# The last expert's first tile of rows, weighed and scattered in two halves of its columns

## The chip, the cores and the metric

The kernel runs on one core of a Trainium2 chip. The metric is the device time of one execution in microseconds. All arithmetic on the main path is in float32.

## What is computed

An attention block without a softmax is followed by a mixture of experts that leaves some rows alone. Cut to what matters here:

```python
kv  = einsum('bhsd,bhse->bhde', k, v)
o   = einsum('bhsd,bhde->bhse', q, kv)
x   = o / sqrt(mean(o*o, -1) + 1e-6) * g_norm     # rows: 4608 x 512
out = x.copy()
for the rows with x @ w_skip > 0:
    e      = argmax(x @ w_gate)                   # one of 8 experts
    gate_w = softmax(x @ w_gate)[e]
    h      = relu(x @ w1[e])                      # 512 -> 1024
    out[row] = x + gate_w * (h @ w2[e])           # 1024 -> 512
```

## The kernel before

The first part of the program computes x, writes it to the output in DRAM, and gives every chosen row a slot at its expert. The second part goes through the experts one after the other, those with most rows first (`experts`, L1428). For each expert, GpSimd gathers the rows from DRAM into a tile `xg` (128 partitions; a chunk `c` of 512 columns holds one row on each partition), TensorE turns them, multiplies by w1 (layer 1), and multiplies the hidden values by w2 (layer 2). What comes out of layer 2 for a tile of 128 rows stands in one PSUM bank of 128 x 512 values. VectorE weighs it: a `scalar_tensor_tensor` computes `x = gate * bank + x` in `xg` (in `result`, L1381). GpSimd then scatters the rows to their places in DRAM with an indirect DMA (L1384), which takes the row numbers from a table.

Layer 2 for the first 256 rows of an expert is `fast_2` (L1326). It uses a scheme of Winograd's kind: the 256 rows, the hidden values and the columns are halved, and seven products of half size take the place of eight, with some sums on VectorE in between. `X` is the bank of the first tile of rows and `Y` that of the second; `lo` and `hi` are the two halves of a bank's columns, 256 each. A product (`product`, L1251) is four matmuls over the hidden values, which the trace shows as eight records each of matmul and of weight load. The order in which the source issues the work is the order on every engine (the schedule is written out by hand), so TensorE does these products one after the other as they stand in `fast_2`: X lo, Y lo, X hi, Y lo again, X lo again (L1361), X hi again (L1363), and Y lo a last time (L1368). X hi gets an `add` (L1364) before it is final. `held` copies half a bank to SBUF on ScalarE.

`put` calls `result` for a whole tile. `part` is a second way out of a bank, used in the last expert alone (r = E - 1, L1488): it calls `half_result` (L1400), which weighs one half of the columns (L1404) and scatters it as half rows of 256 values (L1407). Its row numbers, twice the row number plus the half, come from the table `two`, built by `half_rows` (L1391) in the second expert's turn for both tiles and both halves. Before the change, only Y goes out this way: its `hi` half right after its add (L1359) and its `lo` half after the very last product (L1370). X goes out whole through `put` (L1365). The last expert has exactly 256 rows of room, so `rest` (L1366) is empty for it, and it has no sums of a next expert to do (`do(work, ...)` finds an empty list).

All scatters of one pass stand in a group within which the program declares no order between them (L1388, L1411), since each row has one slot. GpSimd issues them in the order of the source.

Of the kernel before, what the change touches and what calls it, by code (L numbers as in the profile page):

```python
# [17 lines left out]
def kernel(  # L18
# [47 lines left out]
    P = 128  # L66
# [940 lines left out]
    for n in range(NU + 2):  # L1007
# [31 lines left out]
        for pace, stream in streams:  # L1039
            for job in itertools.islice(stream, pace):  # L1040
                if job:
                    part, job = job if isinstance(job, tuple) else ("pe", job)
# [9 lines left out]
    with tc.tile_pool(name="wpool_b", bufs=1, reuse_waits="tile") as wpool_b, \  # L1052
# [6 lines left out]
        def bank():  # L1059
            return ps_b.tile([P, 512], FP32, tag="bank", name="bank")  # L1060
# [116 lines left out]
        def layer_2(r, ht, piece, yps=None, fs=range(FC)):  # L1177

            off, m = piece[0:2]
            n = DM * m // P  # L1180
            ht = ht if callable(ht) else (lambda f, all=ht: all[:, f, :])
            yps = yps or bank()
            for f in fs:
                for q in range(P // m):
                    nc.tensor.matmul(out=yps[q * m:(q + 1) * m, 0:n], lhsT=ht(f)[:, off:off + m],  # L1185
                                     rhs=w_sb[r][1][:, f, q * n:(q + 1) * n],
                                     start=(f == 0), stop=(f == FC - 1), skip_group_check=True)
            return yps
# [56 lines left out]
        def do(work, n=None):  # L1245
            n = len(work) if n is None else min(n, len(work))
            for job in work[:n]:
                job()
            del work[:n]

        def product(out, k, lhsT, rhs, start):  # L1251
            for i in range(k):
                nc.tensor.matmul(out=out, lhsT=lhsT(i), rhs=rhs(i), start=start and i == 0,  # L1253
                                 stop=i == k - 1, skip_group_check=True)

        def add(to, x, y):
            nc.vector.tensor_tensor(out=to, in0=x, in1=y, op=ALU.add)  # L1257

        def held(x, tag):

            n = x.shape[-1]
            t = ffn.tile([P, 256], FP32, tag=tag, name=tag)[:, 0:n]
            nc.scalar.copy(out=t, in_=x)  # L1263
            return t
# [61 lines left out]
        def fast_2(r, ht, rest, work, put, part=None):  # L1326

            w2, s, t = w_sb[r][1], sums.pop((r, "h")), sums.pop((r, "w2"))
            lo, hi = slice(0, HM), slice(HM, DM)

            def h(j, m):
                return lambda f: ht[:, j * HF + f, m * P:(m + 1) * P]

            def hs(i):
                return lambda f: s[:, i, f, :]

            def w(j, ds):
                return lambda f: w2[:, j * HF + f, ds]

            def ws(i):  # L1340
                return lambda f: t[:, i, f, :]

            X, Y = bank(), bank()
            product(X[:, lo], HF, h(0, 0), w(0, lo), True)
            p1 = held(X[:, lo], "p1")
            do(work, 3)
            product(Y[:, lo], HF, hs(1), ws(1), True)
            add(Y[:, lo], Y[:, lo], p1)  # L1350
            u = held(Y[:, lo], "u")
            do(work, 3)
            product(X[:, hi], HF, hs(0), ws(0), False)
            p5 = held(X[:, hi], "p5")
            do(work, 2)
            product(Y[:, lo], HF, h(0, 1), ws(2), False)
            add(Y[:, hi], Y[:, lo], p5)
            if part:
                part(1, 1, Y)  # L1359
            do(work, 2)  # L1360
            product(X[:, lo], HF, h(1, 0), w(1, lo), False)  # L1361
            do(work, 2)
            product(X[:, hi], HF, hs(2), w(1, hi), False)  # L1363
            add(X[:, hi], X[:, hi], u)  # L1364
            put((0, P), X)  # L1365
            for piece in rest:  # L1366
                put(piece[0:2], layer_2(r, ht, piece))
            product(Y[:, lo], HF, h(1, 1), ws(3), False)  # L1368
            if part:
                part(1, 0, Y)  # L1370
            else:
                put((P, P), Y)
            do(work)
# [54 lines left out]
        def experts(pieces, widths, srcs, xt, ht, yps0, tables, group):  # L1428

            for r in range(E):  # L1430
# [36 lines left out]
                if r == 0:  # L1467
                    if yps0 is None:
                        gather_all(2, pieces, *srcs)
                    ys = [bank() for _ in todo]  # L1470
                    for fs in (range(HF), range(HF, FC)):
                        for piece, y in zip(todo, ys):
                            layer_2(r, ht, piece, y, fs)
                    do(beside, 4)
                    for piece, y in zip(todo, ys):
                        result(piece, y, xgs[r], tables, group)
                    do(beside)
                else:
                    if yps0 is not None and r == 1:
                        rnd_i = rounds()  # L1480
                    if yps0 is not None and r == E - 1:
                        n_rounds.append(nc.values_load(rnd_i[0:1, 0:1], min_val=1,
                                                       max_val=ROUNDS + 1))
                    of = {piece[0:2]: piece for piece in todo}
                    part = None
                    if yps0 is not None and r == 1:
                        two = half_rows(tables[0][0])
                    if yps0 is not None and r == E - 1:  # L1488
                        part = lambda c, half, y: half_result(c, half, y, xgs[r], two,
                                                              tables[0][1], group)  # L1490
                    fast_2(r, ht, todo[2:], beside,
                           lambda key, y: result(of[key], y, xgs[r], tables, group), part)
# [136 lines left out]
```

## Time and profile before

| | us |
|---|---|
| time, median of 3 runs | 376.25 (375.22 to 376.61) |
| the profiled execution's own time | 376.26 |
| its span, first to last instruction | 374.40 |
| TensorE busy in matmuls | 363.2 |
| VectorE busy | 244.3 |
| ScalarE busy | 146.0 |
| GpSimd busy | 123.1 |

The span is shorter than the time, since the time takes in what lies before the first and after the last instruction. In the profile, PE is TensorE's matmuls and PEld its weight loads, which overlap them; DVE is VectorE, ACT is ScalarE, POOL is GpSimd. A row names the line, the engine, the operation, the tiles written and read by the program's names (all PSUM tiles of the second part are called `bank`), and in square brackets how long the engine had been idle and whose work ended that. The ends of matmuls are modelled. The granted clock of TensorE was 0.996 of full speed over the span.

The rows that matter for the change are those of the last 12 us. Layer 2 of the last expert begins on TensorE at 356.6 us. The last scatter of the program starts at 370.05 us and takes GpSimd 0.98 us; the rest of the span, to 374.40, is the landing of its bytes and the end of the program.

### The profile page before, as it was taken

To read this page: it belongs to the slowest core of one execution; us is meant where nothing else is said; L and a number is where in the kernel's file an instruction comes from. 1 tells how busy PE (TensorE), PEld (TensorE's weight loads), DVE (VectorE), ACT (ScalarE), POOL (GpSimd) and SP (SyncE) were. 2 spreads that over 40 slices of the span, in tenths; PEclk is the share of its full clock that TensorE was granted. 3 is DMA by queue.
4 is the path that set the end of the run, shared out by engine and by line. 5 is a ranking of instruction groups with operands and counts; after the bars stand their busy time and mean duration, and the time that the engine had idled before them with its cause. 6 is when DMAs were issued, how large, how long until landed. Compare 5 with 4: busy or idle time off the path is not lost.

```text
span 374.4 us, 9661 instructions
## 1 busy us (share of the span) xinstructions
PE 363.2 (97%) x3859; PEld 315.2 (84%) x3859; DVE 244.3 (65%) x627; ACT 146.0 (39%) x398; POOL 123.1 (33%) x191
## 2 busy tenths in 40 slices
PE   8999999999999999999999999999999999999994
PEld 4687797898979679779879987988998998998983
DVE  2354458667878845676766675876876876878831
ACT  2366676676776222214403421430440440441420
POOL 7035457655768555223012303203202302102003
PEclk9999999999999999999999999999999999999998
DMA  7999999996499449966518263672762761700001
GB/s 290 393 391 391 401 403 394 404 384 201 130 330 311 111 109 325 395 204 226 203 53 268 69 226 103 225 254 54 259 228 47 273 230 61 269 3 32 26 1 53
DMA packets 32039, 81.70 MB, mean 218 GB/s; under 512 B 2474, under 2 KB 2482, under 8 KB 31988
## 3 DMA queue, kind: packets, MB, share of 16 engines
q1 hardware_dynamic: 28176, 69.47, 52.3%
q0 software_dynamic: 3792, 11.53, 9.2%
q8 instruction: 32, 0.52, 0.6%
q14 instruction: 19, 0.16, 0.1%
q10 hardware_dynamic: 20, 0.02, 0.0%
HBM read 66.80 MB, written 14.48 MB: 217 GB/s over the span
## 4 chain that ended last, share of the span: by engine, by line
PE 83%; issue 6%; POOL 4%; DVE 3%; ACT 3%; POOLq 0%; DVEq 0%; ACTq 0%
PE bank L1253 44%; PE bank L1185 9%; PE o_ps L498 7%; PE sum_ps L379 5%; PE bank L1173 4%; PE q_ps L460 3%; PE g_ps L393 2%; PE q_ps L170 2%; PE bank L1154 2%; POOL xb L615 2%; DVE xl L545 1%; DVE rs L522 1%; PE g_ps L411 1%; ACT qT L463 1%; ACT sq L514 1%
## 5 line engine op out<-in xcount | busy, mean ns | idle before, releaser
L1263 ACT COPY p<-bank 128x128 f32<-128x128 f32 (+6 forms) x70 | 20.8, 297 | 99.5 <-PE bank L1253 88.2
L1253 PE MATMUL bank<-xt,w 128*128 128x128 f32 (+5 forms) x336 | 55.5, 288 | 0.0
L615 POOL TENSOR_TENSOR xb<-xl,g_b 128x512 f32<-128x512 f32 x36 | 43.7, 1216 | 34.3 <-DVE rs L536 30.4
L1384 POOL DMA_INDIRECT out_dram<-xg,rows x14 | 14.0, 999 | 118.6 <-DVE xg L1381 115.4
L1253 PEld LDWEIGHTS bank<-xt,w 128*128 128x128 f32 x336 | 47.0, 190 | 1.9 <-DVE bank L1257 1.4
L1257 DVE TENSOR_TENSOR bank<-bank,p 128x128 f32<-128x128 f32 (+6 forms) x70 | 23.6, 338 | 30.2 <-PE bank L1253 29.0
L498 PE MATMUL o_ps<-kvd,qT 128*128 128x146 f32 x240 | 35.8, 290 | 1.0 <-ACT kvd L415 0.7
L1253 PE MATMUL bank<-xs,s 128*128 128x128 f32 (+5 forms) x224 | 36.7, 289 | 0.0
L522 DVE TENSOR_REDUCE rs<-sq 128x8 f32<-128x512 f32 x36 | 24.6, 682 | 15.6 <-ACT sq L514 15.5
L498 PEld LDWEIGHTS o_ps<-kvd,qT 128*128 128x128 f32 x240 | 31.6, 188 | 2.0 <-ACT kvd L415 1.5
L1253 PEld LDWEIGHTS bank<-xs,s 128*128 128x128 f32 x224 | 31.1, 190 | 1.0 <-ACT p L1263 0.8
L1185 PE MATMUL bank<-w,ht 128*32 128x128 f32 (+2 forms) x424 | 29.9, 313 | 0.0
L545 DVE TENSOR_TENSOR xl<-o_ps,rs 128x584 f32<-128x584 f32 x32 | 24.5, 767 | 4.3 <-DVE rs L536 0.5
L1185 PEld LDWEIGHTS bank<-w,ht 128*32 128x32 f32 (+2 forms) x424 | 18.2, 119 | 10.7 <-issue 7.6
L1253 PE MATMUL bank<-t,ht 128*128 128x256 f32 x112 | 27.0, 384 | 0.0
L1145 POOL DMA_INDIRECT xg<-out_dram,src x14 | 15.6, 1116 | 33.3 <-DMA out_dram<-xg,rows 18.0
L1253 PE MATMUL bank<-w,ht 128*128 128x256 f32 x112 | 26.5, 380 | 0.0
L514 ACT ACTIVATE sq<-o_ps 128x512 f32<-128x512 f32 x34 | 20.3, 597 | 15.0 <-PE o_ps L498 14.4
L379 PE MATMUL sum_ps<-v,k 64*64 64x64 f32 x1152 | 25.3, 227 | 0.4 <-issue 0.4
L1253 PE MATMUL bank<-t,hs 128*128 128x256 f32 x112 | 25.3, 379 | 0.0
L379 PEld LDWEIGHTS sum_ps<-v,k 64*64 64x64 f32 x1152 | 21.4, 138 | 4.5 <-issue 2.2
L1253 PEld LDWEIGHTS bank<-t,ht 128*128 128x128 f32 x112 | 20.8, 190 | 3.9 <-issue 1.2
(223 smaller groups left out, 679.2 us busy)
## 6 DMA issues: line engine op xcount, KB each, us to landing
w<-in_moe_w_dram SPq DMA_DIRECT2D x16, 2048.0 KB, 8.9
k<-in_k_dram SPq DMA_DIRECT2D x16, 576.0 KB, 9.9
v<-in_v_dram SPq DMA_DIRECT2D x16, 576.0 KB, 10.7
q<-in_q_dram SPq DMA_DIRECT2D x16, 576.0 KB, 10.2
out_dram<-xb SPq DMA_DIRECT2D x29, 256.0 KB, 9.8
out_dram<-xb POOLq DMA_DIRECT2D x7, 256.0 KB, 6.6
xg<-out_dram,src POOLq DMA_INDIRECT x16, 3.6
out_dram<-xg,rows POOLq DMA_INDIRECT x16, 6.2
```

Of the source, the lines that this page charges most:

```text
L379: nc.tensor.matmul(out=sum_ps[w * 64:(w + 1) * 64, a, u, :], lhsT=kt[r, 2 * u + w, c, :], rhs=vt[r, 2 * u + w, c, :], start=(c == 0), stop ...
L498: mm = nc.tensor.matmul(out=ps[:, w, 0:2 * PK].rearrange("p (r k) -> p r k", r=2)[:, :, cols], lhsT=qT[:, w, a, :], rhs=kvds[b % KVD][:, u ...
L514: nc.scalar.activation(out=sq[:, :, :, :], in_=heads(ps, G, G + 2 * D), func=ACT.Square)
L522: nc.vector.tensor_reduce(out=rs[:, :, :], in_=sq[:, :, :, :].rearrange("p x y (a d) -> p x (y a) d", a=2), axis=AX.X, op=ALU.add)
L545: nc.vector.tensor_tensor(out=xl[:, :, :, :].rearrange("p x y (a k) -> p x (y a) k", a=2), in0=ps[:, :, 0:2 * PK].rearrange("p x (h k) -> ...
L615: late.append((lambda: nc.gpsimd.tensor_tensor(out=xb[:, :, 4 * u * D:(4 * u + 4) * D].rearrange("p r (w x) -> p r w x", w=2), in0=xl[:, : ...
L1145: nc.gpsimd.indirect_dma_start(out=x_of(xg, off, m), out_offset=None, in_=cut_rows(m)[:, :], in_offset=bass.IndirectOffsetOnAxis(ap=idx[:, ...
L1173: nc.tensor.matmul(out=hps[:, cols], lhsT=w_sb[r][0][:, dc, f * P:(f + 1) * P], rhs=xt[:, dc, cols], start=(dc == 0), stop=(dc == DC - 1))
L1185: nc.tensor.matmul(out=yps[q * m:(q + 1) * m, 0:n], lhsT=ht(f)[:, off:off + m], rhs=w_sb[r][1][:, f, q * n:(q + 1) * n], start=(f == 0), s ...
L1253: nc.tensor.matmul(out=out, lhsT=lhsT(i), rhs=rhs(i), start=start and i == 0, stop=i == k - 1, skip_group_check=True)
L1257: nc.vector.tensor_tensor(out=to, in0=x, in1=y, op=ALU.add)
L1263: nc.scalar.copy(out=t, in_=x)
```

## The change

In the last expert, X also goes out in two halves. Its `lo` half is weighed and scattered directly after the second product into X lo, ahead of the product into X hi; its `hi` half is weighed and scattered after the add, where `put` sent out the whole tile. In all other experts `part` is None and nothing differs.

```diff
             do(work, 2)
             product(X[:, lo], HF, h(1, 0), w(1, lo), False)
+            if part:
+                part(0, 0, X)
             do(work, 2)
             product(X[:, hi], HF, hs(2), w(1, hi), False)
             add(X[:, hi], X[:, hi], u)
-            put((0, P), X)
+            if part:
+                part(0, 1, X)
+            else:
+                put((0, P), X)
             for piece in rest:
                 put(piece[0:2], layer_2(r, ht, piece))
             product(Y[:, lo], HF, h(1, 1), ws(3), False)
```

What `part` calls was there before:

```python
        def half_result(c, half, yps, xg, two, gate, group):
            ds = slice(half * HM, (half + 1) * HM)
            col = (E - 1) * CK + c
            nc.vector.scalar_tensor_tensor(
                out=xg[:, c, ds], in0=yps[:, ds], scalar=gate[:, col:col + 1], in1=xg[:, c, ds],
                op0=ALU.mult, op1=ALU.add)
            ins = nc.gpsimd.indirect_dma_start(
                out=cut_rows(P // 2)[:, :],
                out_offset=bass.IndirectOffsetOnAxis(ap=two[:, c, half:half + 1], axis=0),
                in_=xg[:, c, ds], in_offset=None, bounds_check=2 * N - 1, oob_is_err=False)
            tc.declare_no_dep(ins.ins, group=group, reason="each row has one slot")
            tc.add_to_no_dep_group(group, ins.ins)
```

## The prediction

> **What bounds the kernel now.** I read the page's first and fourth part, then the timeline of the last 25 us, since the changed lines run once, in the last expert, then the timelines of two earlier places where TensorE waits for another engine's access to a PSUM bank, and last the windows and landings of the final stores. The page first:
>
> ```profile
> PE 363.2 (97%) x3859; PEld 315.2 (84%) x3859; DVE 244.3 (65%) x627; ACT 146.0 (39%) x398; POOL 123.1 (33%) x191
> ...
> PE 83%; issue 6%; POOL 4%; DVE 3%; ACT 3%; POOLq 0%; DVEq 0%; ACTq 0%
> ```
>
> TensorE is the bound nearly throughout: 97% busy and 83% of the chain that ended last. Any wait added on TensorE ahead of its last matmul moves the end almost one for one, unless something after it has slack. Whether it has, the timeline of the end shows (start us, us, engine, line, operation, names, shapes, count, idle before and who ended it):
>
> ```profile
> 363.61 1.89 PE L1253 MATMUL bank<-w,ht 128*128 128x256 f32 x8
> 363.88 0.43 DVE L1257 TENSOR_TENSOR bank<-bank,p 128x256 f32<-128x256 f32 x1 [3.02 <-PE bank L1253]
> 364.34 0.48 DVE L1404 SCALAR_TENSOR_TENSOR xg<-bank,gate,xg 128x256 f32<-128x256 f32 x1
> 365.10 0.98 POOL L1407 DMA_INDIRECT out_dram<-xg,rows  x1 [19.43 <-DVE xg L1404]
> 365.12 1.70 PEld L1253 LDWEIGHTS bank<-w,hs 128*128 128x128 f32 x8
> 365.33 1.89 PE L1253 MATMUL bank<-w,hs 128*128 128x256 f32 x8
> 366.84 1.70 PEld L1253 LDWEIGHTS bank<-t,ht 128*128 128x128 f32 x8
> 367.06 1.89 PE L1253 MATMUL bank<-t,ht 128*128 128x256 f32 x8
> 367.26 0.43 DVE L1257 TENSOR_TENSOR bank<-bank,u 128x256 f32<-128x256 f32 x1 [2.43 <-PE bank L1253]
> 367.73 0.75 DVE L1381 SCALAR_TENSOR_TENSOR xg<-bank,gate,xg 128x512 f32<-128x512 f32 x1
> 368.76 0.98 POOL L1384 DMA_INDIRECT out_dram<-xg,rows  x1 [2.67 <-DVE xg L1381]
> 368.99 0.48 DVE L1404 SCALAR_TENSOR_TENSOR xg<-bank,gate,xg 128x256 f32<-128x256 f32 x1 [0.51 <-PE bank L1253]
> 370.05 0.98 POOL L1407 DMA_INDIRECT out_dram<-xg,rows  x1 [0.30 <-issue]
> ```
>
> Three products of eight matmul records end it: X lo (363.61 to 365.50), X hi (365.33 to 367.22), Y lo (367.06 to 368.95); each starts 1.73 us after the one before. X is finished by an add (L1257), weighed whole (L1381, 512 columns, 0.75 us) and scattered at 368.76. Y lo is weighed from 368.99 to 369.47. A scatter starts 0.28 us after the weighing it waits for (364.82 to 365.10; 368.48 to 368.76), so Y lo's could start at 369.75. It starts at 370.05, because GpSimd is in X's scatter until 369.74 and the next one follows 0.31 us later. So the end is set by X's chain through GpSimd's queue, with Y lo's own chain 0.30 us behind. After that last scatter ends at 371.03, 3.37 us remain to the span's end at 374.40.
>
> The windows of the end say whether the bytes matter:
>
> ```profile
> 369.70:370.00 0.30, 0.00 (x0) 0.00 (x0) 0.00 (x0) 0.00 (x0) 0.04 (x1) 1.00 0.00 0
> ...
> 370.30:370.60 0.30, 0.00 (x0) 0.00 (x0) 0.00 (x0) 0.00 (x0) 0.30 (x1) 1.00 1.08 369
> 370.60:370.90 0.30, 0.00 (x0) 0.00 (x0) 0.00 (x0) 0.00 (x0) 0.30 (x1) 1.00 0.98 355
> ...
> 371.50:371.80 0.30, 0.00 (x0) 0.00 (x0) 0.00 (x0) 0.00 (x0) 0.00 (x0) 0.50 0.69 256
> ```
>
> The last two columns are DMA share and GB/s. X's 256 KB move at 370.3 to about 371.0, Y lo's 128 KB at about 371.4 to 371.9: the engines are free again before the last scatter's bytes come, so moving X's bytes earlier shortens nothing behind it.
>
> **What the Trainium skill says.** "PSUM — Partial Sum Buffer", section "PSUM bank collisions raise a hardware error": two engines must not access one bank and partition quadrant at the same time, even at disjoint columns, and the guard is to be by bank, not by address. X lo and X hi are two halves of one bank, and the new weighing reads X lo while TensorE's next product writes X hi. The trace of before shows that this kernel is guarded so. At an expert's start, ACT copies X lo, and the product into X hi of the same bank waits for that read:
>
> ```profile
> 232.21 0.27 ACT L1263 COPY p<-bank 128x134 f32<-128x134 f32 x1 [10.79 <-PE bank L1253]
> 232.53 0.53 PEld L1253 LDWEIGHTS bank<-xs,s 128*128 128x128 f32 x4 [0.16 <-ACT p L1263]
> ```
>
> and with VectorE, at the end of layer 1, the product into X lo waits for the add on X hi (355.11 + 0.30 = 355.41; weights at 355.47):
>
> ```profile
> 355.11 0.30 DVE L1257 TENSOR_TENSOR bank<-bank,u 128x128 f32<-128x128 f32 x1
> 355.47 0.52 PEld L1253 LDWEIGHTS bank<-xt,w 128*128 128x128 f32 x4 [0.21 <-DVE bank L1257]
> ```
>
> In both, the weight load begins 0.05 to 0.06 us after the other engine ends; it waits too, so nothing is preloaded. "SBUF — State Buffer", section "Who interferes with whom": a VectorE instruction with one SBUF input does not contend with GpSimd. The trace agrees: L1404 takes 0.48 us alone (364.34) and inside a scatter (368.99). "DMA: Bandwidth & Descriptors", section "Anatomy of one DMA", puts a fixed cost of about 2.0 us on a GpSimd DMA, mostly completion; here issue to landing was 2.9, 3.2 and 2.4 us for the last three scatters, so it stays a constant behind the last one.
>
> **The change part by part.**
>
> Added: one L1404 weighing of X lo straight after its product, and its scatter. VectorE is idle then (364.82 to 367.26), so its own 0.48 us is free there: 365.54 to 366.02, starting 0.04 us after the product's end as at 368.95 to 368.99. Its scatter would be ready at 366.30; GpSimd is in Y hi's until 366.08, plus 0.31 makes 366.39, to 367.37. GpSimd is idle until 368.76 now, so its 0.98 us is hidden.
>
> Added wait: the X hi product is the next thing on TensorE's queue and, by the rule above, stands until 366.02; Y lo stands behind it, and both of their weighings and scatters behind that. Weight load at 366.02 + 0.05 = 366.07; from an idle array the first matmul follows its load by about 0.10 us (at 355.47 the four that follow end at 356.18, and four take 0.61), so 366.17 in place of 365.33. Stall 0.84 us. From below it would be 0 (no wait at all); from above 0.95, taking the slowest start of a VectorE instruction after a product here (0.11, 363.77 to 363.88) and rounding. I take 0.84.
>
> Removed: L1381 on 512 columns (0.75) becomes L1404 on 256 (0.48): 0.27 us less on X's chain, and half its bytes.
>
> The sum: X hi ends 367.22 + 0.84 = 368.06; add 368.10 to 368.53; weighing 368.57 to 369.05; scatter 369.33 to 370.31. Y lo ends 369.79; weighing 369.83 to 370.31, so its scatter could start at 370.59; GpSimd is free for it at 370.31 + 0.31 = 370.62. It starts at 370.62, against 370.05: +0.57, which is 0.84 less 0.27. Ends 371.60; plus the unchanged 3.37 gives a span of 374.97. The half rows' address table and both of Y's halves are there already; nothing before the last expert's X lo changes.
>
> The profiled execution took 376.26 us, 1.86 more than its span of 374.40, and equals the median of the runs, 376.25. So the forecast is 376.25 + 0.57 = 376.8 us.
>
> **The rivals.**
>
> A, no wait by bank: the weighing overlaps the X hi product. X hi's scatter then starts 0.27 earlier, 368.49 to 369.47; Y lo's is ready at 369.75, the queue free at 369.78. Gain 0.27: 376.0 us. For it: the columns are disjoint. Against it: the two waits shown, and that the summary of waits counts twelve of TensorE's weight loads behind these two rows (five on ACT's p, seven on L1257's bank).
>
> B, the other side: the weighing of X hi writes columns of xg beside those that X lo's scatter is still reading, and waits for that scatter's landing. It starts at 366.39 and lands 2.4 to 3.2 us later, 368.8 to 369.6; a wait on a landing cost a further 0.6 earlier (scatter at 164.80, 6.7 to landing, the gather behind it started at 172.37, less 0.28 of issue). The weighing would start at 369.4 to 370.2 in place of 368.57, Y lo's scatter at 371.5 to 372.3 (0.48 + 0.28 + 1.29 later): +1.4 to +2.2, so 377.7 to 378.5, about 378.1 us. It decides as soon as a landing comes after 368.0. Against it: Y lo's weighing at 368.99 writes columns of the same xg while X's scatter, begun at 368.76, reads others, and it starts 0.04 us after its product. That speaks for guards on xg by columns.
>
> C, GpSimd as the bound: four scatters at 1.29 us each could queue. But X lo's ends at 367.37, 1.96 us before X hi's wants to start. Only the last pair touches (0.03 us, in the sum). It gives no time of its own unless a scatter of half rows took over 2.9 us, where L1407 shows 0.98.
>
> **How the numbers follow.** Forecast 0.82, A 0.09, B 0.06, 0.03 for what I don't see. The forecast's own spread is 0.48 to 0.68 us; the runs of before spread from 375.22 to 376.61, which is more, so 375.7 to 377.8 holds the forecast with that spread and A, and touches B. 0.5% (about what a measurement of this kernel can tell from no change) is 1.88 us: only B's upper half and the unseen lie beyond. Slower 0.06, faster 0.03, same 0.91. In direction I expect slower by 0.15%, below that bound.
>
> **What would show it.** In the profile of after: an L1404 row near 365.5 of 0.48 us; a TensorE gap of about 0.67 us after X lo (365.50 to 366.17), its release put down to that row; L1404 four times, no L1381 on 512 columns in the last expert; the last scatter near 370.6. Wrong if the X hi product starts at 365.3 (A), if the weighing of X hi starts more than 0.1 us after its add (B), or if the time from the last scatter's end to the span's end isn't 3.4 us.

## The result and the profile after

| | before | after |
|---|---|---|
| time, median of 14 runs each | 375.90 us (374.97 to 377.15) | 377.06 us (376.14 to 377.91) |
| ratio after / before | | 1.0026, 95% interval 1.0015 to 1.0036 |
| profiled execution: time, span | 376.26, 374.4 us | 376.25, 374.5 us |
| last scatter's start, from the start of the second X lo product | 6.44 us | 7.01 us |

The change makes the kernel slower by 0.26%, about 0.98 us (0.56 to 1.35); the two medians lie 1.16 us apart. It was forecast as slower by 0.57 us, too little to be told from no change; the sign is clear only because 14 runs of each were compared.

On the page nothing of this shows. Busy time by engine, and the chain that ended last, after:

```profile
PE 362.1 (97%) x3859; PEld 314.4 (84%) x3859; DVE 244.3 (65%) x628; ACT 146.0 (39%) x398; POOL 124.1 (33%) x192
...
PE 80%; issue 6%; POOL 4%; DVE 3%; ACT 3%; DMA 2%; SPq 0%; POOLq 0%; DVEq 0%; ACTq 0%
```

One more instruction on VectorE, one more on GpSimd with its 1.0 us; in the chain TensorE has 80% where it had 83, and a DMA 2% that wasn't there, which is no measure of a change of 0.26%.

The two profiled executions took the same time, but they can't be compared by their ends: the one of after was 0.69 us ahead when the second X lo product began (362.92 against 363.61), long before anything that the change touches. Single runs of either kernel lie more than 1.7 us apart. What the change does has to be read as distances from that product. The timeline of after, from there on:

```profile
362.92 1.89 PE L1253 MATMUL bank<-w,ht 128*128 128x256 f32 x8
...
364.85 0.48 DVE L1409 SCALAR_TENSOR_TENSOR xg<-bank,gate,xg 128x256 f32<-128x256 f32 x1 [0.71 <-PE bank L1253]
365.38 1.59 PEld L1253 LDWEIGHTS bank<-w,hs 128*128 128x128 f32 x8 [0.98 <-DVE xg L1409]
365.38 1.99 PE L1253 MATMUL bank<-w,hs 128*128 128x256 f32 x8 [0.57 <-DVE xg L1409]
365.71 0.98 POOL L1412 DMA_INDIRECT out_dram<-xg,rows  x1 [0.30 <-issue]
...
367.42 0.43 DVE L1257 TENSOR_TENSOR bank<-bank,u 128x256 f32<-128x256 f32 x1 [2.09 <-PE bank L1253]
367.89 0.48 DVE L1409 SCALAR_TENSOR_TENSOR xg<-bank,gate,xg 128x256 f32<-128x256 f32 x1
368.64 0.98 POOL L1412 DMA_INDIRECT out_dram<-xg,rows  x1 [1.96 <-DVE xg L1409]
369.14 0.48 DVE L1409 SCALAR_TENSOR_TENSOR xg<-bank,gate,xg 128x256 f32<-128x256 f32 x1 [0.78 <-PE bank L1253]
369.93 0.98 POOL L1412 DMA_INDIRECT out_dram<-xg,rows  x1 [0.30 <-DVE xg L1409]
```

(The weighing is line 1409 here, the scatter 1412.) VectorE weighs X lo 0.04 us after the product's end. The weight load of the X hi product starts at 365.38, 0.05 us after that weighing ends, and the brackets put its idle time down to it. Its matmuls begin in the record with that load and take 1.99 us in place of 1.89, so the gap on TensorE reads 0.57 us and not 0.67 as forecast. X hi ends at 367.37, 4.45 us after the start of X lo; before it was 3.61 (363.61 to 367.22), so TensorE lost 0.84 us. The weighing of X hi follows its add without a wait, 0.27 us shorter than the whole tile's. The last scatter starts 7.01 us after X lo began, 0.57 later than before.

That leaves the end. From the last scatter's end to the span's end there were 3.37 us before (371.03 to 374.4) and 3.59 after (370.91 to 374.5); the spans are given to 0.1 us, so such a stretch is good to about 0.05. The sum had taken this for unchanged. The first two rows of GpSimd's clean-up after the landing, and the wait behind them (engine queue, operation, count, shortest, middle and longest ns, first and last start). Before, in the views of the two last source lines:

```profile
L1579 POOLq INC_SWDGE_SEM  x1: 248/248/248, 372.5 to 372.5; - x1
L1624 POOLq DRAIN  x3: 51/113/299, 372.8 to 374.0; - x3
L1624 POOLq EVENT_SEMAPHORE  x4: 17/17/17, 373.5 to 374.3; - x4
```

After:

```profile
L1584 POOLq INC_SWDGE_SEM  x1: 268/268/268, 372.5 to 372.5; - x1
L1629 POOLq DRAIN  x3: 51/113/381, 372.8 to 374.1; - x3
L1629 POOLq EVENT_SEMAPHORE  x4: 17/17/17, 373.6 to 374.4; - x4
```

The first row takes 20 ns more, the longest drain, the first of the three, 82 ns. Every later profile with four scatters in the last expert has 268 and 381 too, every one with three 248 and 299. The two can't be added up: GpSimd goes on only at 373.5 and 373.6, some 0.4 us after that drain has ended in either kernel, when SyncE signals. From the start of INC_SWDGE_SEM to the end of the span the traces have 1.90 to 1.91 us in all eight profiles with three scatters and 1.92 in all six with four: in the clean-up a fourth scatter costs 0.02 us. The expectations below count 0.1 for it, which is too much.

### The profile page after: what moved, and what is told of

Same layout as the page of the kernel before. It is cut to its first block, busy times and chain, and to the rows that moved or that the text cites. A ratio compares the mean times of both kernels' runs of the same rounds, so it can differ in the third digit from the quotient of the medians.

```text
span 374.5 us, 9666 instructions
## 1 busy us (share of the span) xinstructions
PE 362.1 (97%) x3859; PEld 314.4 (84%) x3859; DVE 244.3 (65%) x628; ACT 146.0 (39%) x398; POOL 124.1 (33%) x192
## 4 chain that ended last, share of the span: by engine, by line
PE 80%; issue 6%; POOL 4%; DVE 3%; ACT 3%; DMA 2%; SPq 0%; POOLq 0%; DVEq 0%; ACTq 0%
PE bank L1253 44%; PE bank L1185 9%; PE o_ps L498 7%; PE sum_ps L379 4%; PE bank L1173 4%; PE q_ps L460 3%; PE g_ps L393 2%; DMA v<-in_v_dram 2%; PE bank L1154 2%; POOL xb L615 2%; POOL out_dram L1412 1%; DVE xl L545 1%; DVE rs L522 1%; PE g_ps L411 1%; ACT qT L463 1%
## 5 line engine op out<-in xcount | busy, mean ns | idle before, releaser
L1389 POOL DMA_INDIRECT out_dram<-xg,rows x13 | 13.0, 1001 | 115.2 <-DVE xg L1386 112.0
```

## The experiments

Theory 1: the cost is TensorE's wait for the bank of X, less what the shorter weighing saves. Theory 2: it is the fourth scatter, in GpSimd's queue or after the last scatter. In the table, "start" is the last scatter's start counted from the start of the first of the last three products, "tail" is from its end to the end of the span; both from one profile each. Ratios are to the kernel before on the same chip, with its times as 1.

| kernel | scatters | start, us | tail, us | ratio, 95% interval |
|---|---|---|---|---|
| before | 3 | 6.44 | 3.37 | |
| before again | 3 | 6.44 | 3.51 | 0.9999 (0.9984 to 1.0015) |
| after | 4 | 7.01 | 3.59 | 1.0026 (1.0015 to 1.0036) |
| after again | 4 | 7.02 | 3.90 | 1.0028 (1.0015 to 1.0040) |
| bank of its own | 4 | 6.17 | 3.60 | 1.0002 (0.9990 to 1.0015) |
| wait alone | 3 | 7.28 | 3.52 | 1.0039 (1.0026 to 1.0053) |
| X lo late | 4 | 7.47 | 3.98 | 1.0051 (1.0031 to 1.0071) |
| one scatter of X | 3 | 7.01 | 3.70 | 1.0024 (1.0007 to 1.0041) |
| short wait | 3 | 7.04 | 3.40 | one run |
| double wait | 3 | 7.67 | 3.52 | one run |
| X hi first | 4 | 6.14 | 4.43 | 1.0021 (1.0009 to 1.0033) |
| X hi first, three scatters | 3 | 6.15 | 4.84 | 1.0025 (1.0015 to 1.0035) |
| X hi first, Y's rows last | 4 | 6.14 | 4.55 | 1.0021 (1.0009 to 1.0033) |
| bank of its own, one scatter of X | 3 | 6.16 | 3.43 | 0.9991 (0.9979 to 1.0003) |

**A bank of its own.** The change is kept, but X hi's products go to another bank.

```diff
             X, Y = bank(), bank()
+            Z = bank() if part else X
...
-            product(X[:, hi], HF, hs(0), ws(0), False)
+            product(Z[:, hi], HF, hs(0), ws(0), Z is not X)
...
-            product(X[:, hi], HF, hs(2), w(1, hi), False)
-            add(X[:, hi], X[:, hi], u)
+            product(Z[:, hi], HF, hs(2), w(1, hi), False)
+            add(Z[:, hi], Z[:, hi], u)
             if part:
-                part(0, 1, X)
+                part(0, 1, Z)
```

> The changed kernel, with X hi of the last expert in a PSUM bank of its own, so that weighing X lo and the product into X hi touch different banks. Theory 1 (the cost is TensorE's wait for the bank): the X hi product follows X lo without a gap, the last scatter starts 0.27 us earlier than in the kernel before, counted from the start of the X lo product (6.17 us after it, against 6.44 before and 7.01 with the change); time about 0.3 us below before. Theory 2 (the fourth scatter costs, in GpSimd's queue or in the landing of the half rows): the last scatter starts as early, but the stretch from its end to the end of the span is 3.6 us as with the change, not 3.4, and the time is level with before or some tenths above.

Its timeline (X lo's product begins at 363.75):

```profile
365.48 1.89 PE L1253 MATMUL bank<-w,hs 128*128 128x256 f32 x8
365.68 0.48 DVE L1410 SCALAR_TENSOR_TENSOR xg<-bank,gate,xg 128x256 f32<-128x256 f32 x1 [0.70 <-PE bank L1253]
...
369.92 0.98 POOL L1413 DMA_INDIRECT out_dram<-xg,rows  x1 [0.30 <-DVE xg L1410]
```

The X hi product begins before X lo's weighing and runs beside it: no bracket, no gap. The same weighing on the same data holds TensorE up only if it reads the bank that TensorE writes next. (Each PSUM tile of this program is one bank, so a guard by bank and a guard by tile look the same here; which of the two the program's waits follow, these runs do not tell.) The last scatter starts 6.17 us after X lo. The time falls by about 0.9 us against the change, to that of before, but not below it: 0.27 us are won before the last scatter, and the tail is 3.60, as theory 2 said of it, against 3.37 and 3.51 in the two profiles of before. The interval, some 0.5 us to either side, can't tell such tenths apart.

**The wait alone.** The kernel before, with a read of X lo that serves nothing at the changed place: `aside` weighs X lo as `half_result` does, into a scratch tile.

```diff
             product(X[:, lo], HF, h(1, 0), w(1, lo), False)
+            if part:
+                aside(X)
             do(work, 2)
```

> The kernel before, with one more weighing of X lo into a scratch tile at the place of the change; the result of it is not used, X is weighed and scattered whole as before. Theory 1: TensorE waits as with the change, and the 512-column weighing stays, so the last scatter starts 0.84 us later than before (7.28 us after the start of the X lo product); time +0.8 us. Theory 2: three scatters only, so the excess of the change over its sum (0.98 measured, 0.57 in the sum) is missing here: time +0.4 us or less.

The last scatter is at 7.28, to the hundredth as the sum has it. The time, +1.5 us (1.0 to 2.0), is more than the 0.84: theory 2's lower value is out, and even the lower end of the interval lies 0.1 us above theory 1's value. What this rest of about 0.6 us is, I can't say; its one profile has a tail of 3.52, which holds 0.2 of it at most. This kernel has three scatters, so a time above the sum is not by itself a sign of the fourth.

Two kernels change the length of that read, to 32 columns and to twice 256.

```diff
-            out=t[:, :], in0=yps[:, 0:HM], ... in1=xg[:, 0, 0:HM]
+            out=t[:, 0:32], in0=yps[:, 0:32], ... in1=xg[:, 0, 0:32]
```

```diff
+                aside(X)
                 aside(X)
```

> The kernel before with a weighing of only 32 columns of X lo into a scratch tile at the place of the change; its result is not used. Theory 1, the wait priced as the duration of VectorE's instruction plus a fixed 0.36 us (0.84 less 0.48): L1404 shows 0.48 us for 256 columns and the rows of 128 columns 0.13 less, so some 0.25 for 32, a stall of 0.61, the last scatter 7.05 us after the start of the X lo product. If the price goes with the columns read: 0.1 us of stall, 6.55.

> The kernel before with the weighing of X lo into scratch done twice at the place of the change; the results are not used. Two weighings back to back took 0.87 us in the kernel with X lo late, so the second adds 0.39. Theory 1: stall 1.23 us, the last scatter 7.67 us after the start of the X lo product. If TensorE waited only for a fixed hand-over, 7.28 as with one.

The timelines, 32 columns first:

```profile
366.21 0.25 DVE L1405 SCALAR_TENSOR_TENSOR p<-bank,gate,xg 128x32 f32<-128x32 f32 x1 [0.70 <-PE bank L1253]
366.51 1.59 PEld L1253 LDWEIGHTS bank<-w,hs 128*128 128x128 f32 x8 [0.74 <-DVE p L1405]
```

```profile
365.16 0.88 DVE L1406 SCALAR_TENSOR_TENSOR p<-bank,gate,xg 128x256 f32<-128x256 f32 x2 [0.71 <-PE bank L1253]
366.09 1.59 PEld L1253 LDWEIGHTS bank<-w,hs 128*128 128x128 f32 x8 [1.37 <-DVE p L1406]
```

An eighth of the columns still takes 0.25 us and delays the end by 0.60 (7.04 less 6.44); two reads delay it by 1.23. The price of such a wait is VectorE's time plus 0.35 to 0.36 us: with one read of 256 columns that is 0.04 to its start, 0.05 to the weight load, 0.17 by which two products following each other overlap in the record (365.33 to 365.50 before), and 0.10 that the product behind the wait takes longer (1.99 for 1.89).

**X lo late.** The change, with X lo's weighing after the add, so that TensorE waits for nothing.

```diff
-            if part:
-                part(0, 0, X)
             do(work, 2)
             product(X[:, hi], HF, hs(2), w(1, hi), False)
             add(X[:, hi], X[:, hi], u)
             if part:
+                part(0, 0, X)
                 part(0, 1, X)
```

> The changed kernel with X lo weighed and scattered only after the add on X hi, next to X hi: no wait added on TensorE, but all four scatters. Theory 1: no gap on TensorE; GpSimd becomes the bound, two scatters of X and Y lo's one behind the other at 1.29 us each: X lo's starts 4.88 us after the start of the X lo product, X hi's at 6.17, Y lo's at 7.46, which is +1.02 us on before; time +1.0 us. If the wait were all there is, and scatters cheap: time level with before.

Its timeline (X lo begins at 364.07):

```profile
368.96 0.98 POOL L1411 DMA_INDIRECT out_dram<-xg,rows  x1 [2.40 <-DVE xg L1408]
...
370.25 0.99 POOL L1411 DMA_INDIRECT out_dram<-xg,rows  x1 [0.30 <-DVE xg L1408]
371.54 0.98 POOL L1411 DMA_INDIRECT out_dram<-xg,rows  x1 [0.30 <-issue]
```

Three scatters stand one behind the other at 1.29 us. The last one starts at 7.47, as forecast, and this is the slowest of all. So the fourth scatter is free only where GpSimd has a gap for it, and the place that the change picked gives it one; it is paid for with TensorE's wait instead.

**One scatter of X.** The change, with X scattered once after both weighings.

```diff
+            if c == 0:
+                if half == 0:
+                    return
+                ins = nc.gpsimd.indirect_dma_start(
+                    out=cut_rows(P)[:, :],
+                    out_offset=bass.IndirectOffsetOnAxis(ap=rows[:, col:col + 1], axis=0),
+                    in_=xg[:, c, :], in_offset=None, bounds_check=N - 1, oob_is_err=False)
...
+                return
```

> The changed kernel with both weighings of X where they are, but X scattered once and whole after the second: three scatters as in the kernel before. Theory 1: the last scatter starts where it does with the change (7.01 us after the start of the X lo product), time +0.57 us on before. Theory 2: the excess over the sum goes, that is, the time is some tenths below that of the change and the stretch after the last scatter's end is 3.4 us again, not 3.6.

The start is that of the change. The ratio, 1.0024, is not to be told from 1.0026. The clean-up rows went back to 248 and 299 ns, the tail in this profile did not go down to 3.4 (3.70). By the time alone this experiment decides nothing; its tail speaks against theory 2.

**X hi first.** The last three products in another order, so that each weighing lies beside a product into the other bank; nothing else is changed.

```diff
+            if part:
+                product(X[:, hi], HF, hs(2), w(1, hi), False)
+                add(X[:, hi], X[:, hi], u)
+                part(0, 1, X)
+                product(Y[:, lo], HF, h(1, 1), ws(3), False)
+                part(1, 0, Y)
+                product(X[:, lo], HF, h(1, 0), w(1, lo), False)
+                part(0, 0, X)
+                return
```

> The changed kernel with the last three products of the last expert in another order: X hi, Y lo, X lo, each followed by its weighing and half-row scatter. Same banks as before. Theory 1 (the wait for the bank is the cost): the add and the weighing of X hi lie beside the Y lo product, which writes the other bank, so TensorE doesn't wait; the last scatter starts 6.14 us after the start of the first of the three products, against 6.44 in the kernel before and 7.01 with the change. Four scatters lengthen the clean-up at the end by 0.1 us (0.02 + 0.08 on two GpSimd rows, as in the four-scatter profiles so far), so the time is 0.2 us below before and about 0.8 below the change. If something else than the wait costs (the scatters, the halves): level with the change.

> The same order of products, with Y weighed in halves but scattered once and whole after Y lo: three scatters. Theory 1: the last scatter starts at 6.14 us again, the clean-up is as in the kernel before (rows of 248 and 299 ns, not 268 and 381), so the time is 0.3 us below before. If a fourth scatter costs more than its 0.1 us, this kernel gains more on the one with four.

A miss, and the clearest one. The last scatter starts at 6.14 and 6.15 us, as forecast, TensorE has no gap, and yet both kernels are 0.2% slower than before. All of it is in the tail, 4.4 and 4.8 us: about 1.1 us more than the others' 3.5 with three scatters, less 0.3 won, makes the measured 0.8 to 0.9. The rows of the queues at the program's last branch, for the kernel with four scatters, whose last product ends at 370.29 and last scatter at 372.07:

```profile
L1585 PEldq COMPARE_BRANCH  x1: 3350/3350/3350, 367.9 to 367.9; - x1
L1585 PEldq EVENT_SEMAPHORE  x1: 51/51/51, 371.3 to 371.3; - x1
L1585 POOLq INC_SWDGE_SEM  x1: 268/268/268, 374.6 to 374.6; - x1
```

and for the kernel before, whose last product ends at 368.95 and last scatter at 371.03:

```profile
L1579 PEldq COMPARE_BRANCH  x1: 3450/3450/3450, 364.9 to 364.9; - x1
L1579 PEldq EVENT_SEMAPHORE  x1: 51/51/51, 369.0 to 369.0; - x1
```

GpSimd begins its clean-up 2.5 us after the last scatter's end, where it took 1.5 before. TensorE's branch takes some 3.4 us in both; before, it is over 0.6 us before the last product ends, here 1.0 us after that. It starts later here because TensorE's queue has a wait close to the end: the last product writes the bank that X hi's weighing reads, and the branch starts 0.1 us after the end of that weighing (367.83).

With X hi first, the last scatter carries X's rows, and the last expert has 211 rows for these inputs: X fills all 128 slots, Y only 83. One more kernel tells whether the rows are it.

```diff
-                out=xg[:, c, ds], in0=yps[:, ds], scalar=..., in1=xg[:, c, ds],
+                out=xg[:, 1 if half == 0 else c, ds], in0=yps[:, ds], scalar=...,
+                in1=xg[:, 1 if half == 0 else c, ds],
                 op0=ALU.mult, op1=ALU.add)
+            if half == 0:
+                c = 1 - c
```

> The kernel with X hi, Y lo, X lo in that order and four scatters, with the last two scatters exchanged: the third writes X lo's half rows (128 rows, not yet weighed), the last writes Y lo's (the last expert has 211 rows, so 83 of Y's 128 slots are filled), into which the weighing after X lo goes. Left out: the weighed values of X lo; Y lo's half rows get them on top. Instructions, order and waits are those of the kernel with X hi first. Theory R (a scatter with all 128 rows lands later than one with 83): last scatter 6.14 us after the start of the first of the three products, and from its end to the end of the span 3.4 to 3.9 us again, time 0.2 us below before or level with it. Theory O (the other order of products makes the end late, by what the engines do at their last branch): 4.4 to 4.8 us again, time +0.2% on before.

The tail stays at 4.55 us and the ratio at 1.0021: theory R falls, the number of rows isn't it. It is the order.

The traces also hold every DMA packet, and these show where the tail comes from. INC_SWDGE_SEM waits for the last scatter's landing. Counted from the last scatter's end, in us:

| profiles | its last packet ends | from there to the end of the span |
|---|---|---|
| old order, three scatters (7) | 1.08 to 1.33, mean 1.14 | 2.26 to 2.39 |
| old order, four scatters (4) | 1.15 to 1.55, mean 1.33 | 2.39 to 2.46 |
| X hi first (3) | 1.95, 2.42, 1.98 | 2.46, 2.38, 2.57 |

In the three kernels with X hi first, all packets of the last scatter but two (its closing ones of 4 bytes aside) are over by 1.1 us. A packet of 16 KB in the queue that the page calls "instruction" ends at 1.25, 1.72 and 1.46 us, and in each of the three the first of the two late packets starts within 0.02 us of that end. In all 14 profiles such a packet starts 0.7 to 1.3 us after TensorE's branch has ended; in the kernel before that was early enough for it to be over 0.7 and 0.1 us before the last scatter's end. So the late branch and the other transfer belong together: the branch comes late, its 16 KB come late, and by these times the last two packets are held up behind them. They fit in all three; a kernel that moves the branch alone was not run.

**Before and after again.**

> The kernel before, unaltered, once more: how far a ratio strays when nothing is changed, and a second profile of its end. Theory 1: ratio 1.000 within 0.001; last scatter at 6.44 us after the start of the X lo product; the stretch from the last scatter's end to the span's end somewhere from 3.4 to 3.9 us, if that spread is the landing's own. Theory 2 (the half rows slow the landing): 3.4 us again.

> The changed kernel, unaltered, once more, beside the others on one chip. Theory 1: last scatter 7.01 us after the start of the X lo product, time +0.57 from the sum and +0.1 from the clean-up of the fourth scatter, about +0.7 us. If the excess of the first measurement (+0.98) is a cost of its own, about +1.0 us again.

The kernel before reads 0.9999 against itself, with an interval of 0.0015 to either side; that is the grain of all the ratios above. Its tail was 3.51 this time. The change reads 1.0028, +1.06 us, so the first +0.98 was no accident, and its tail is 3.90. Both are above the +0.7 expected, though their intervals take it in.

**A bank of its own and one scatter of X.** The two edits together; the lines that carry them:

```diff
+            Z = bank() if part else X
...
+            product(Z[:, hi], HF, hs(2), w(1, hi), False)
...
+                    in_=xg[:, c, :], in_offset=None, bounds_check=N - 1, oob_is_err=False)
```

> The kernel with a bank of its own for X hi, with X weighed in halves but scattered once and whole after X hi: no wait on TensorE, three scatters. Theory 1: last scatter 6.17 us after the start of the X lo product (0.27 less than before), clean-up as in the kernel before, 0.1 less than with four scatters, so 0.3 us below before; 0.1 us below the kernel with its own bank and four scatters. If the gain goes into the landing: level with before.

Start 6.16, tail 3.43, and the only altered kernel whose ratio has its middle below 1: 0.9991, about 0.34 us, with an interval that just takes in 1. It beats the change; that it beats the kernel before, the profile says by 0.28 us, and the times alone do not show it.

## Why the prediction held, and the term that was too small

**The wait.** Right in mechanism and size. The prediction took from two earlier places of the trace that this program keeps TensorE out of a bank that another engine reads, at other columns too, and priced the stall at 0.84 us. It measured 0.84. The own bank shows that sharing the bank is the cause, the wait alone that the wait suffices to stop TensorE, and the two other lengths how it is priced.

**The weighing and the queue.** Right: 0.48 for 0.75 us, the fourth scatter in GpSimd's gap, the last pair touching. The last scatter moved by 0.57 us, as summed.

**"Plus the unchanged 3.37".** This is the term that was too small, and by the prediction's own sign ("isn't 3.4 us") it was wrong. The tail isn't a constant. The prediction's own three landings, 2.9, 3.2 and 2.4 us, had said so; it took the last for fixed all the same. Two profiles of before have 3.37 and 3.51, two of after 3.59 and 3.90, some 0.3 us more in the mean. With it the sum is about 0.9 us, inside both measured intervals (0.56 to 1.35 and 0.57 to 1.51); the forecast 0.57 stands at the lower edge of both.

Is it the fourth scatter? With the products in the old order, the seven profiles with three scatters have 3.37 to 3.70 us, 3.49 in the mean, the four with four scatters 3.59 to 3.98, 3.77 in the mean: 0.28 us between the means, of single profiles whose ranges overlap. Only 0.02 of it is the clean-up; most of the rest is the moment at which the last scatter's last packet ends (1.14 and 1.33 us in the mean). In X lo late, which has the latest of these, 1.55, a packet of the last scatter started just as an 8 KB packet of the instruction queue ended, at 1.19 us. With X hi first the kernel with three scatters has the longer tail, 4.84 against 4.43. So what else the DMA queues carry at that moment moves the tail at least as much as the number of scatters, and that the fourth scatter as such lengthens it is not shown beyond the 0.02. TensorE's wait may have a part in it: it also moved the start of TensorE's branch from 1.3 to 2.6 us after the start of X lo, and the 16 KB packet behind it closer to the last scatter. The runs do not settle this.

**Bytes.** The last scatter was read as 128 KB. Its packets carry 83 rows, 85 KB; nothing in the sum hangs on it.

**The level.** 376.8 was forecast and 377.06 measured, which is closer than it deserves and in part luck: the forecast started from the median of three runs, 376.25, and 14 runs gave 375.90. The level was 0.35 too high, the step between the medians 0.59 too low (0.41 by the ratio).

**The rivals.** A (no wait by bank) fell: the X hi product starts 0.05 us after the weighing, not before it. Its saving is real, but needs another bank. B (the weighing of X hi waits for X lo's scatter) fell: it starts at 367.89, 0.04 us after its add ends, while X lo's scatter, begun at 365.71, has not landed: the four landings of after took 2.3 to 3.2 us, so this one came at 368.0 at the earliest. C (GpSimd as the bound) is not what happens here, and is what happens as soon as X lo's scatter has no gap, as X lo late shows with +1.03 us of start.

## What to carry to other kernels

Before a read of a finished half of a PSUM bank is moved ahead of a matmul into the other half, look where the trace makes TensorE wait for reads of that bank: here it costs the reader's time plus about 0.35 us, for 32 columns as for 256. Another bank for the second half takes the wait away. And when the order of work at the end of a program changes, measure the stretch from the last store's issue to the end in several profiles before calling it fixed, and look at what else the DMA queues carry while the last store lands.

## What the runs showed of the hardware

- One more GpSimd scatter lengthened the clean-up at the program's end by 0.02 us, in all six profiles with four scatters against all eight with three. Its longest drain took 381 ns for 299, but this was hidden behind a wait for SyncE.
- The landing of the last scatter is not a constant of its size: with four scatters and 83 rows in the last one, its last packet ended 1.15 and 1.40 us after the scatter in the two profiles of after and 1.98 us after it in another order of products, behind a 16 KB packet of the instruction queue.
- Timings between two fixed points of one program, such as a product and a scatter, repeated to 0.01 us in profiles of the same kernel (6.44 twice; 7.01 and 7.02), while the times of whole runs of these two kernels spread by 1.8 to 3.2 us. A change of half a microsecond is read in the first and only then confirmed in the second.
